# Expert products in four widths: TensorE branches on the token count of an expert

## Chip, cores, metric

The kernel runs on one core of a Trainium2 chip. The metric is device microseconds (us) of one execution, as the median of several runs; lower is better.

## The reference

Gated linear attention over 4 batches, 8 heads and 768 steps feeds a mixture of 8 experts, of which each token uses one, and a dense gated layer follows. What matters here is the mixture: 3,072 tokens of 384 features, each sent to the expert with the largest logit.

```python
logits = x @ w_gate
expert_idx = np.argmax(logits, axis=1)
...
for e in range(E):
    mask = expert_idx == e
    xe = x[mask]
    h = np.maximum(xe @ w1[e], 0.0)        # 384 -> 1024
    ye = h @ w2[e]                         # 1024 -> 384
    out[mask] = gate_w[mask, None] * ye
```

How many tokens an expert gets is known only when the attention has run. The inputs are drawn from a fixed seed, so the counts can be had from the reference itself: expert 0 gets 420 tokens, and the other seven, sorted, get 409, 404, 390, 387, 356, 354 and 352.

## The kernel before

The program has three stages. The attention, with the routing, runs to about 131 us of the profiled span; the experts run from there to about 369 us; the dense layer fills the rest. TensorE (PE) does the products; ScalarE (ACT) and VectorE (DVE) turn PSUM into the next operands; GpSimd (POOL) gathers tokens and splits some weights; SyncE (SP) issues the loads.

**Turns and capacities.** The experts are taken in turns. Turn 0 is expert 0, which starts on its first 192 tokens before the last batch has been routed; turns 1 to 7 are the others by falling count, sorted on the chip (`turns`). Since an instruction's size is fixed when the program is built, each turn works on as many columns (tokens) as its capacity in `CAPS` says: 448 for turn 0, then 464, 436, 420, 408, 396, 384, 370. A count above its capacity sends the whole call to a slow general path behind the `tc.If` at the end (line 1547).

**Products.** An expert is cut into 8 slices of 128 inner units. For slice `t` of 64, `F1` computes the inner units: nine products (`first`, line 1222), because each operand is split into a high and a low part and three of the four partial products are kept, over three blocks of 128 features; the result lies in a PSUM bank `hp`. ACT makes `hh` from it (line 1234) and DVE makes `hl` (line 1236). `S1` (line 1254) then multiplies `hh` and `hl` by the second weights, again nine products, into three accumulators `yb`, which are emptied into `yT` at the end of an expert (`y_store`, lines 1398 and 1400). A product is one weight load and one matmul of as many columns as the capacity.

**The order around the change** is written out by hand, in the loop from line 1478. It takes the slices in pairs (g0, g1): `F1` of g1, then weight splitting (`doubles`, `weights`), `F1` of the slice after the pair, transposes of gathered tokens for the next expert (`x_tile`, line 357), and `S1` of g0 and of g1. Each `F1` is followed at once by its `hh` on ACT and its `hl` on DVE, so those two sit in the middle of the other work of these in-order engines. `hp` alternates between two PSUM banks, 5 and 6 (`h_bank`); `hh` and `hl` have two buffers each. A few list steps (`late`: `offsets`, `turn_lists` and others) are dropped in, one per slice. `offsets` (lines 1322 to 1329) writes the first row of each turn into `regs`, from which engines load registers with `values_load`.

Of the kernel before, what the change touches and what calls it, by code (L numbers as in the profile page):

```python
# [35 lines left out]

CAPS = [448, 464, 436, 420, 408, 396, 384, 370]
CAP = max(CAPS)
CA = 192
NTILE = NT // 128  # L40
RING = 5
# [188 lines left out]
def gla_moe_kernel(  # L230
# [883 lines left out]
    with mctx:  # L1114
# [112 lines left out]
                        step()  # L1227

        def F1(t, c0, c1, mid=()):
            n = c1 - c0  # L1230
            hp = bank(h_bank(), [128, TM], "hp")[:, :n]
            first(wslot[slot1(t)], XT[t // NF], c0, c1, hp, mid)
            hh = mp.tile([128, TM], F32R, tag="hh", name="hh", bufs=2)
            nc.scalar.activation(hh[:, :n], hp, AF.Relu)  # L1234
            hl = mp.tile([128, TM], F32R, tag="hl", name="hl", bufs=2)
            nc.vector.scalar_tensor_tensor(  # L1236
                hl[:, :n], in0=hp, scalar=0.0, in1=hh[:, :n].bitcast(F32), op0=ALU.max, op1=ALU.subtract
            )
            hq[t, c0] = (hh, hl)
# [1 line left out]
        yb = {}  # L1241

        def S1(t, c0, c1, between=()):
            f = t % NF
            if f == 0 and c0 == 0:
                for dc in range(KD):
                    yb[dc] = bank(dc, [128, CAP], "yb")
            wh, wl = wslot[slot1(t)]
            hh, hl = hq.pop((t, c0))
            for dc in range(KD):  # L1250
                c = 384 + dc * 128
                i = 0
                for a, b_ in ((wh, hh), (wl, hh), (wh, hl)):
                    nc.tensor.matmul(  # L1254
                        yb[dc][:, c0:c1],
                        lhsT=a[:, c : c + 128],
                        rhs=b_[:, : c1 - c0],
                        start=(f == 0 and c0 == 0 and i == 0),
                        stop=(f == NF - 1 and i == 2),
                    )  # L1260
                    i += 1
                if dc < len(between):
                    between[dc]()
# [23 lines left out]
        for t in range(part):  # L1287
            if t == 2:
                add()
                w_split(4)  # L1290
                gather(0, (1, 2, 3))
            if t == 3:
                w_split(5)
            if t + 1 < part:
                F1(t + 1, 0, CA)
            for step in beside.get(t, []):
                step()
            if t == part - 2:
                x_tile(0, 1, CA - 128)
            if t == part - 1:  # L1300
                x_tile(0, 2, bk=4)
            S1(t, 0, CA, ([row[2], ranks_and, row[4]], [lambda: None, invert])[t] if t < 2 else [])
            if t == 0:
                row[5]()
                for step in placed:
                    step()
        x_tile(0, 3, bk=3)
        for t in range(4, 6):
            next_load()
        soon = [6, 7]  # L1310
        F1(*seq[0])
        lctx.close()
        wC = mctx.enter_context(tc.tile_pool(name="wC", bufs=1, reuse_waits="tile"))
# [8 lines left out]
        def offsets():  # L1322
            m = rt.tile([128, E, E], F32, tag="m8", name="m8", bufs=1)
            nc.vector.tensor_tensor(inc8, carry, e512, op=ALU.subtract)
            by_turn(inc8, m, cnt)
            nc.vector.tensor_tensor_scan(inc8, ones8, cnt, 0.0, op0=ALU.mult, op1=ALU.add)
            o = rt.tile([128, E], F32, tag="rk", name="o", bufs=1)
            nc.vector.tensor_tensor(o, inc8, cnt, op=ALU.subtract)
            nc.vector.tensor_copy(regs[:, 0:E], o)

        def read_offset(e):
            return nc.values_load(regs[0:1, e : e + 1], engines=(ET.Activation, ET.DVE), min_val=0, max_val=NT)
# [35 lines left out]
            nc.sync.dma_start(slot_d[0:NT].rearrange("(i p) o -> i (p o)", p=128), t[0:NTILE, 2, :])  # L1368

        def turn_lists():  # L1370
            t = bank(3, [4 * E, 128], "tr")
            nc.tensor.transpose(t, ttab, ident)
            nc.vector.tensor_copy(lists["to"], t)

# [7 lines left out]
            nc.sync.dma_start(lists["back"], slot_d[0:NT].rearrange("(i p) o -> i (p o)", p=128))  # L1382

        def turn_slots():
            t = bank(3, [128, NTILE], "tb")
            nc.tensor.transpose(t, lists["back"], ident[:NTILE, :NTILE])
            nc.vector.tensor_scalar(sidx, t, float(NT - 1), None, op0=ALU.min)

# [19 lines left out]
            nc.vector.tensor_tensor(xl[:, kc, :], src, xh[:, kc, :].bitcast(F32), op=ALU.subtract)  # L1408

        def F2(g):  # L1410
            if g >= NM * NF2:
                return
            if g == 0:
                HB[0], HBS[:] = -1, [4, 5, 6]
            m, f = divmod(g, NF2)
            hp = bank(h_bank(), [128, TM], "hp")
            first(wslot[slot2(f)], XT["m", m], 0, TM, hp)
            sg = mp.tile([128, TM], F32, tag="sg", name="sg", bufs=2)
# [58 lines left out]

        for i in range(0, len(seq), 2):
            (g0, *_), (g1, *_) = pair = seq[i : i + 2]
            F1(*seq[i + 1])  # L1480
            doubles(g0, 1)
            if g0 >= RING:
                weights(g0 + 3)
            doubles(g0)
            if g1 >= RING:
                weights(g1 + 3)
            F1(*seq[i + 2]) if i + 2 < len(seq) else F2(0)
            if soon:
                w_split(soon.pop(0))
                next_load()  # L1490
            for g in (g0, g1):
                e, f = divmod(g, NF)
                if f == NF - 2:
                    roff[e] = read_offset(e)
                if f in (1, 2, 3, 4):
                    x_tile(e + 1, f - 1, bk=7 if f % 2 else 4)
                if f in (2, 3, 4, 5):
                    gather(e + 2, (f - 2,))
                if g >= 2 and f < NF - 1 and late:
                    late.pop(0)()  # L1500
                if e == E - 1 and f in (2, 3, 4):
                    y_split(0, f - 2)
            doubles(g1)
            for g, c0, c1 in pair:
                S1(g, c0, c1)
                if g % NF == NF - 1:
                    y_store(g // NF)
        NG2 = NM * NF2
        checks = []
        for p in range(NP + 1):  # L1510
# [101 lines left out]
```

## Time and profile before

| what | value |
|---|---|
| median of 3 runs | 771.36 us (770.86 to 772.2) |
| the profiled execution | 772.25 us, of which 770.2 us are the span of the trace |
| PE busy | 756.6 us, 98% of the span |
| DVE, ACT, POOL busy | 61%, 48%, 21% |
| granted TensorE clock | 0.998 of full speed |

The page gives busy time by engine and by group of instructions, and the trace behind it can be asked for waits, for a stretch in order of time, or for one line. All times are counted from the start of the span. "PEld" is a weight load, "PEldq" or "DVEq" the sequencer of an engine, which handles branches, register loads and separate waits ahead of the work that the engine is doing.

### The profile page before, as it was taken

The page shows a single profiled execution, that of the slowest core. Times are in us where ns is not written, and L with a number is a line of the kernel's source. Part 1 is how long each engine was busy: PE and PEld are TensorE (multiplying, and loading weights), DVE is VectorE, ACT ScalarE, POOL GpSimd, SP SyncE. Part 2 cuts the span into 40 slices and gives each one's busy share as a digit, 9 for nine tenths or more (in the row PEclk, how much of TensorE's full clock was granted, in tenths as well). Part 3 has the DMA queues.
Part 4 walks back from the last instruction along what each step waited for, and adds up shares of the span by engine and source line. Part 5 has one row for each costly group of instructions (what it writes and reads, how often), then busy time and mean ns, then how long its engine had stood idle before and what let it go on. Part 6 is the DMA issues. An engine that isn't in the chain of part 4 may idle for free. (4 is left out here: it accounts for less than half of the span.)

```text
span 770.2 us, 13235 instructions
## 1 busy us (share of the span) xinstructions
PE 756.6 (98%) x5018; PEld 690.6 (90%) x5018; DVE 468.2 (61%) x771; ACT 366.1 (48%) x684; POOL 162.3 (21%) x207
## 2 busy tenths in 40 slices
PE   7999999999999999999999999999999999999997
PEld 6887877898999999999999899999989999898996
DVE  8989986657777787879688433333443333344222
ACT  1656566345554555555544334444554545334222
POOL 5764322321232222212121200020020001002002
PEclk9999999999999999999999999999999999999999
DMA  9797883544455465555111100030021101001001
GB/s 231 200 240 223 202 277 126 169 130 149 147 192 184 151 200 176 184 164 165 62 62 37 59 19 19 1 113 18 1 78 37 37 0 42 2 1 41 1 2 45
DMA packets 41776, 80.56 MB, mean 105 GB/s; under 512 B 5696, under 2 KB 19999, under 8 KB 41704
## 3 DMA queue, kind: packets, MB, share of 16 engines
q1 hardware_dynamic: 37704, 67.60, 29.4%
q0 software_dynamic: 4000, 12.03, 5.1%
q8 instruction: 41, 0.67, 0.4%
q14 instruction: 31, 0.25, 0.1%
HBM read 68.04 MB, written 9.47 MB: 101 GB/s over the span
## 5 line engine op out<-in xcount | busy, mean ns | idle before, releaser
L1222 PE MATMUL hp<-xh,wh 128*128 128x512 f32 (+10 forms) x498 | 182.4, 369 | 0.4 <-issue 0.4
L1222 PE MATMUL hp<-xh,wl 128*128 128x512 f32 (+10 forms) x498 | 182.1, 368 | 0.0
L1423 DVE TENSOR_TENSOR sg<-hp,sg 128x512 f32<-128x512 f32 (+1 forms) x97 | 66.5, 685 | 129.4 <-ACT sg L1422 128.9
L1222 PE MATMUL hp<-xl,wh 128*128 128x512 f32 (+10 forms) x498 | 129.4, 368 | 0.0
L1422 ACT ACTIVATE sg<-hp 128x512 f32<-128x512 f32 (+1 forms) x97 | 57.5, 593 | 119.1 <-PE hp L1222 114.1
L1222 PEld LDWEIGHTS hp<-xh,wh 128*128 128x128 f32 x498 | 93.6, 188 | 12.6 <-issue 1.1
L1222 PEld LDWEIGHTS hp<-xh,wl 128*128 128x128 f32 x498 | 93.7, 188 | 11.3
L1222 PEld LDWEIGHTS hp<-xl,wh 128*128 128x128 f32 x498 | 91.1, 188 | 12.6
L1234 ACT ACTIVATE hh<-hp 128x464 fp32r<-128x464 f32 (+9 forms) x70 | 34.1, 488 | 100.0 <-PE hp L1222 61.8
L1468 POOL DMA_INDIRECT out_dram<-o,sidx x24 | 23.3, 973 | 275.4 <-ACT o L1466 270.9
L1149 POOL TENSOR_TENSOR wl<-dx,wh 128x384 fp32r<-128x384 f32 x32 | 38.4, 1201 | 182.6 <-ACT wh L1146 182.6
L333 DVE TENSOR_TENSOR wl<-raw,wh 128x768 fp32r<-128x768 f32 x63 | 64.3, 1025 | 6.7 <-ACT wh L332 6.4
L1236 DVE SCALAR_TENSOR_TENSOR hl<-hp,hh 128x464 fp32r<-128x464 f32 (+9 forms) x70 | 38.5, 550 | 40.3 <-ACT hh L1234 38.2
L1434 DVE TENSOR_TENSOR hl<-sg,hh 128x512 fp32r<-128x512 f32 x49 | 33.9, 692 | 35.6 <-ACT hh L1433 34.2
L1433 ACT CAST hh<-sg 128x512 fp32r<-128x512 f32 x49 | 30.4, 621 | 49.9 <-DVE sg L1423 38.2
L1434 DVE TENSOR_TENSOR xl<-sg,xh 128x512 fp32r<-128x512 f32 (+1 forms) x48 | 32.7, 681 | 31.7 <-ACT xh L1433 21.3
L332 ACT CAST wh<-raw 128x768 fp32r<-128x768 f32 x64 | 51.5, 831 | 0.6 <-DMA raw<-in_wt_dram 0.5
L1254 PE MATMUL both<-hh,wh 128*128 128x420 f32 (+9 forms) x140 | 49.0, 350 | 0.0
L1254 PE MATMUL both<-hl,wh 128*128 128x420 f32 (+9 forms) x140 | 47.3, 338 | 0.0
L1254 PE MATMUL both<-hh,wl 128*128 128x420 f32 (+9 forms) x140 | 47.2, 337 | 0.0
L1433 ACT CAST xh<-sg 128x512 fp32r<-128x512 f32 (+1 forms) x48 | 29.3, 611 | 35.1 <-DVE sg L1423 32.0
L347 POOL DMA_INDIRECT xg<-x_d,gidx x29 | 32.7, 1127 | 39.7 <-PE xt L357 20.3
(363 smaller groups left out, 1647.4 us busy)
## 6 DMA issues: line engine op xcount, KB each, us to landing
raw<-in_wt_dram SPq DMA_DIRECT2D x64, 384.0 KB, 3.5
raw<-in_w_dram SPq DMA_DIRECT2D x32, 384.0 KB, 3.2
raw<-in_alpha_dram SPq DMA_DIRECT2D x16, 336.0 KB, 3.4
x_d<-xr SPq DMA_DIRECT2D x24, 192.0 KB, 1.9
E<-in_q_dram SPq DMA_DIRECT2D x18, 144.0 KB, 5.6
E<-in_k_dram SPq DMA_DIRECT2D x18, 144.0 KB, 3.1
E<-E POOLq DMA_DIRECT2D x18, 114.0 KB
E<-in_q_dram SPq DMA_DIRECT2D x4, 336.0 KB, 10.8
```

The costliest lines, as they stand in the source:

```text
L332: nc.scalar.copy(hi, raw[t])
L333: eng.tensor_tensor(lo, raw.pop(t), hi.bitcast(F32), op=ALU.subtract)
L347: nc.gpsimd.indirect_dma_start(out=x[:n], out_offset=None, in_=src, in_offset=bass.IndirectOffsetOnAxis(ap=idx[:n, i : i + 1], axis=0),)
L1149: nc.gpsimd.tensor_tensor(r["lo"], r["x"], r["hi"].bitcast(F32), op=ALU.subtract)
L1222: nc.tensor.matmul(hp, lhsT=a[:, kc * 128 : (kc + 1) * 128], rhs=x[:, kc, c0:c1], start=(i == 0), stop=(i == 8))
L1234: nc.scalar.activation(hh[:, :n], hp, AF.Relu)
L1236: nc.vector.scalar_tensor_tensor(hl[:, :n], in0=hp, scalar=0.0, in1=hh[:, :n].bitcast(F32), op0=ALU.max, op1=ALU.subtract)
L1254: nc.tensor.matmul(yb[dc][:, c0:c1], lhsT=a[:, c : c + 128], rhs=b_[:, : c1 - c0], start=(f == 0 and c0 == 0 and i == 0), stop=(f == NF - ...
L1422: nc.scalar.activation(sg[:, z], hp[:, z], AF.Sigmoid)
L1423: nc.vector.tensor_tensor(sg[:, z], hp[:, z], sg[:, z], op=ALU.mult)
L1433: nc.scalar.copy(hh[:, z], sg[:, z])
L1434: nc.vector.tensor_tensor(hl[:, z], sg[:, z], hh[:, z].bitcast(F32), op=ALU.subtract)
```

## The change

For turns 1 to 7 the program holds each group of products four times, in widths listed in `ARMS`, the last being the old capacity. PE loads the count of the turn into a register (once per turn) and, ahead of each group, compares it with the widths and jumps to the first that is large enough. There are nine groups in a turn: the first products of slice 0 alone, of slices 1 and 2, 3 and 4, 5 and 6, and of 7 alone, and the second products of four pairs. So there are 63 groups, each with three compares and four arms, and only PE's program has arms. On the other four engines each group leaves one unconditional jump.

```diff
+ARMS = [
+    [448],
+    [420, 432, 444, 464],
+    [404, 412, 420, 436],
+    [388, 396, 408, 420],
+    [376, 388, 396, 408],
+    [364, 376, 384, 396],
+    [344, 356, 368, 384],
+    [326, 342, 354, 370],
+]
...
+        def hold():
+            HB[0] = -1
+            for i in HBS:
+                t = bank(i, [128, CAP], "hp")
+                nc.vector.memset(t, 0.0)
+                held.append(t)
...
+                for t_ in yb.values():
+                    nc.vector.memset(t_[:, CAPS[0] :], 0.0)
...
+        HB[0], HBS[:] = -1, [5, 6, 3]
...
+            nc.vector.tensor_copy(regs[:, 9:16], cnt[:, 1:E])
+        count = {}
+        def sized(e, body):
+            if e not in count:
+                c = 8 + e if e else 8
+                count[e] = nc.values_load(regs[0:1, c : c + 1], engines=(ET.PE,), min_val=0, max_val=NT)
+            def arm(i):
+                if i == len(ARMS[e]) - 1:
+                    body(ARMS[e][i])
+                    return
+                with tc.If(count[e] <= ARMS[e][i]) as cmp:
+                    body(ARMS[e][i])
+                with cmp.Else():
+                    arm(i + 1)
+            arm(0)
...
         for i in range(0, len(seq), 2):
             (g0, *_), (g1, *_) = pair = seq[i : i + 2]
-            F1(*seq[i + 1])
+            todo = seq[i + 1 : i + 3]
+            for t, c0, c1 in todo:
+                F1_bank(t, c0)
...
+                    def firsts(w):
+                        for t, c0, c1 in mine:
+                            F1_products(t, c0, w)
+                    sized(e, firsts)
+            F1_inner(*seq[i + 1])
...
-            F1(*seq[i + 2]) if i + 2 < len(seq) else F2(0)
...
-            for g, c0, c1 in pair:
-                S1(g, c0, c1)
-                if g % NF == NF - 1:
-                    y_store(g // NF)
...
+                sized(e, seconds)
+            if i + 2 < len(seq):
+                F1_inner(*seq[i + 2])
+            else:
+                F2_inner(0)
+            if i == NF - 4:
+                hold()
+            if g1 % NF == NF - 1:
+                y_store(e)
```

Three more things move. `F1` falls into `F1_products` and `F1_inner`: the products of two slices now stand together, and `hh` and `hl` of the second slice come only after the second products of the pair. `hp` lives in three banks (5, 6, 3) that are allocated once and cleared by DVE (`hold`), since a narrow arm leaves the columns behind its width as they were; `turn_lists` and `turn_slots` go to bank 7 for it. ACT and DVE still work on the full capacity.

On PE, the first products of slice 0 of turn 1 (`xh`, `xl` the tokens, `wh_104`, `wl_105` its first weights) stood before between the last of turn 0 and the second products of turn 0:

```order
L1222 MATMUL hp<-xl_108,wh_2031 128x448 x3
L1222 MATMUL hp<-xh_2039,wh_104 128x464
L1222 MATMUL hp<-xh_2039,wl_105 128x464
L1222 MATMUL hp<-xh_2039,wh_104 128x464
L1222 MATMUL hp<-xh_2039,wl_105 128x464
L1222 MATMUL hp<-xh_2039,wh_104 128x464
L1222 MATMUL hp<-xh_2039,wl_105 128x464
L1222 MATMUL hp<-xl_2040,wh_104 128x464 x3
L1254 MATMUL both<-hh,wh_2029 128x448
L1254 MATMUL both<-hh,wl_2030 128x448
```

and now, with the load of the turn's count, the first compare and the first of the four arms:

```order
L1383 TENSOR_LOAD regs
L1383 ISA x2
L1389 COMPARE_AND_BRANCH
L1232 MATMUL hp<-xh_2039,wh_104 128x420
L1232 MATMUL hp<-xh_2039,wl_105 128x420
L1232 MATMUL hp<-xh_2039,wh_104 128x420
L1232 MATMUL hp<-xh_2039,wl_105 128x420
L1232 MATMUL hp<-xh_2039,wh_104 128x420
L1232 MATMUL hp<-xh_2039,wl_105 128x420
L1232 MATMUL hp<-xl_2040,wh_104 128x420 x3
L1389 UNCONDITIONAL_BRANCH
L1389 COMPARE_AND_BRANCH
```

What moved: the nine products stand inside an arm of 420 columns in place of 464, a register load and a compare ahead of them and a jump behind; three more arms of the same nine products follow in the program.

On DVE, at the end of turn 0 (`lists` is the token list, `wl` the low part of a weight, `xl` that of a token block; `hl` of 448 columns belongs to slices 6 and 7), before:

```order
L1236 SCALAR_TENSOR_TENSOR hl<-hp,hh 128x256
L333 TENSOR_TENSOR wl_105<-raw,wh_104 128x768
L1236 SCALAR_TENSOR_TENSOR hl<-hp,hh 128x448
L362 TENSOR_TENSOR xl_2040<-xt,xh_2039 128x3x80
L1373 COPY lists<-tr 32x128
L1236 SCALAR_TENSOR_TENSOR hl<-hp,hh 128x448
L333 TENSOR_TENSOR wl_2026<-raw,wh_2025 128x768
L333 TENSOR_TENSOR wl_99<-raw,wh_98 128x768
L1236 SCALAR_TENSOR_TENSOR hl<-hp,hh 128x464
L1332 TENSOR_LOAD regs
```

and now:

```order
L1272 SCALAR_TENSOR_TENSOR hl<-hp,hh 128x256 x2
L343 TENSOR_TENSOR wl_105<-raw,wh_104 128x768
L372 TENSOR_TENSOR xl_2040<-xt,xh_2039 128x3x80
L1438 COPY lists<-tr 32x128
L1272 SCALAR_TENSOR_TENSOR hl<-hp,hh 128x448
L1256 MEMSET hp 128x464 x3
L1389 UNCONDITIONAL_BRANCH
L1272 SCALAR_TENSOR_TENSOR hl<-hp,hh 128x448
L343 TENSOR_TENSOR wl_2026<-raw,wh_2025 128x768
L343 TENSOR_TENSOR wl_99<-raw,wh_98 128x768
L1389 UNCONDITIONAL_BRANCH
L1397 TENSOR_LOAD regs
```

What moved: `hl` of slice 6 stands behind the token block and the list, and three clears of `hp` follow it, ahead of `hl` of slice 7; a jump marks each group.

## Rows read from the trace of the kernel before

**Rows 1.** The page, parts 1 and 3: busy us, share, instructions; the instruction queue.

```profile
PE 756.6 (98%) x5018; PEld 690.6 (90%) x5018; DVE 468.2 (61%) x771; ACT 366.1 (48%) x684; POOL 162.3 (21%) x207
...
q8 instruction: 41, 0.67, 0.4%
```

**Rows 2.** Waits of PE from 131 to 370 us: total us, times, longest us.

```profile
PE xt L357 <- DMA xg<-x_d,gidx: 0.7, 1, 0.7
PE hp L1222 <- issue: 0.4, 1, 0.4
```

**Rows 3.** Engines in the stretch of turns 1 to 7: length, busy us (instructions) of PE, PEld, DVE, ACT, POOL.

```profile
165.00:370.00 205.00, 205.00 (x1125) 197.08 (x1124) 160.32 (x267) 109.06 (x204) 49.53 (x42) 1.00 0.52 168
```

**Rows 4.** Products of PE in turn 1, in order of time: start us, us.

```profile
177.38 0.38 PE L1254 MATMUL both<-hh,wl 128*128 128x464 f32 x1
...
180.94 0.37 PE L1222 MATMUL hp<-xh,wh 128*128 128x464 f32 x1
```

**Rows 5.** The same in turn 7.

```profile
352.96 0.33 PE L1254 MATMUL both<-hh,wh 128*128 128x370 f32 x1
...
355.51 0.33 PE L1254 MATMUL yb<-hh,wh 128*128 128x370 f32 x1
```

**Rows 6.** Line 1547, the branch at the end: ns min/median/max, first and last start us.

```profile
L1547 SPq EVENT_SEMAPHORE  x8: 17/17/17, 665.6 to 666.1; - x8
L1547 SPq COMPARE_BRANCH  x1: 53/53/53, 663.1 to 663.1; - x1
L1547 PEldq COMPARE_BRANCH  x1: 4015/4015/4015, 761.6 to 761.6; - x1
L1547 DVEq COMPARE_BRANCH  x1: 72/72/72, 765.0 to 765.0; - x1
...
L1547 POOLq COMPARE_BRANCH  x1: 54/54/54, 765.7 to 765.7; - x1
...
L1547 POOLq EVENT_SEMAPHORE  x1: 17/17/17, 765.9 to 765.9; - x1
```

**Rows 7.** The last product of PE, in order of time.

```profile
764.56 0.34 PE L1446 MATMUL ob<-wh,xl 128*128 128x384 f32 x1
```

**Rows 8.** DVE at its branch, in order of time.

```profile
764.94 0.37 DVE L1461 COPY o<-ob 128x200 f32<-128x200 f32 x1 [3.10 <-PE ob L1446]
```

**Rows 9.** Instruction queue of PE from 763 to 766 us: packets, MB, share of 16 engines.

```profile
q8 instruction: 1, 0.02, 1.9%
```

**Rows 10.** Line 357 from 160 to 178 us, the separate waits: count, ns min/median/max.

```profile
L357 PEldq EVENT_SEMAPHORE  x2: 51/819/1587, 160.4 to 173.1; - x2
```

**Rows 11.** PE while the longer of those waits runs, in order of time.

```profile
161.46 0.37 PE L1222 MATMUL hp<-xh,wh 128*128 128x448 f32 x1
161.67 0.36 PE L1222 MATMUL hp<-xh,wl 128*128 128x448 f32 x1
...
163.29 0.35 PE L357 MATMUL xt<-identr,xg 80*128 80x80 f32 x3
```

**Rows 12.** End of turn 0 on DVE, in order of time, with idle time ahead in brackets.

```profile
163.85 0.95 DVE L333 TENSOR_TENSOR wl<-raw,wh 128x768 fp32r<-128x768 f32 x1
165.33 0.62 DVE L1236 SCALAR_TENSOR_TENSOR hl<-hp,hh 128x448 fp32r<-128x448 f32 x1 [0.52 <-ACT hh L1234]
165.87 0.40 DVE L362 TENSOR_TENSOR xl<-xt,xh 128x240 fp32r<-128x240 f32 x1
166.18 0.27 DVE L1373 COPY lists<-tr 32x128 f32<-32x128 f32 x1
```

**Rows 13.** PE and ACT there, all engines in order of time.

```profile
164.75 0.54 ACT L1234 ACTIVATE hh<-hp 128x448 fp32r<-128x448 f32 x1 [1.98 <-PE yb L1254]
...
165.75 0.37 PE L1222 MATMUL hp<-xh,wh 128*128 128x448 f32 x1
```

**Rows 14.** Waits of DVE from 165 to 370 us: total us, times, longest us.

```profile
DVE hl L1236 <- ACT hh L1234: 32.6, 32, 1.9
```

**Rows 15.** The register load of PE ahead of the last branch.

```profile
L1540 PEldq TENSOR_LOAD <-regs x1: 492/492/492, 752.3 to 752.3; - x1
```

More of the change, by code (lines that the diff above doesn't have):

```diff
@@ L1229, in F1, with F1_products, F1_bank, F1_inner @@
         def F1(t, c0, c1, mid=()):
+            F1_bank(t, c0)
+            F1_products(t, c0, c1, mid)
+            F1_inner(t, c0, c1)
+        hps = {}
+        def F1_products(t, c0, c1, mid=()):
+            first(wslot[slot1(t)], XT[t // NF], c0, c1, hps[t, c0][:, : c1 - c0], mid)
+        held = []
+        def hold():
[4 more added lines that the diff above has]
+                held.append(t)
+        def F1_bank(t, c0):
+            if held:
+                HB[0] += 1
+                hps[t, c0] = held[HB[0] % len(held)]
+            else:
+                hps[t, c0] = bank(h_bank(), [128, CAP], "hp")
+        def F1_inner(t, c0, c1):
             n = c1 - c0
-            hp = bank(h_bank(), [128, TM], "hp")[:, :n]
-            first(wslot[slot1(t)], XT[t // NF], c0, c1, hp, mid)
+            hp = hps.pop((t, c0))[:, :n]
             hh = mp.tile([128, TM], F32R, tag="hh", name="hh", bufs=2)
@@ L1243, in S1, with S1_begin, S1_products @@
         def S1(t, c0, c1, between=()):
-            f = t % NF
-            if f == 0 and c0 == 0:
+            S1_products(t, c0, c1, S1_begin(t, c0), between)
+        def S1_begin(t, c0):
+            if t == 0 and c0 == 0:
                 for dc in range(KD):
                     yb[dc] = bank(dc, [128, CAP], "yb")
+            return hq.pop((t, c0))
+        def S1_products(t, c0, c1, inner, between=()):
+            f = t % NF
             wh, wl = wslot[slot1(t)]
-            hh, hl = hq.pop((t, c0))
+            hh, hl = inner
             for dc in range(KD):
@@ L1370, in turn_lists @@
         def turn_lists():
-            t = bank(3, [4 * E, 128], "tr")
+            t = bank(7, [4 * E, 128], "tr")
             nc.tensor.transpose(t, ttab, ident)
@@ L1384, in turn_slots @@
         def turn_slots():
-            t = bank(3, [128, NTILE], "tb")
+            t = bank(7, [128, NTILE], "tb")
             nc.tensor.transpose(t, lists["back"], ident[:NTILE, :NTILE])
@@ L1410, in F2, with F2_products @@
         def F2(g):
-            if g >= NM * NF2:
-                return
+            if g < NM * NF2:
+                F2_products(g)
+                F2_inner(g)
+        def F2_products(g):
             if g == 0:
@@ L1415, in F2, with F2_inner @@
             m, f = divmod(g, NF2)
-            hp = bank(h_bank(), [128, TM], "hp")
+            hps["m", g] = hp = bank(h_bank(), [128, TM], "hp")
             first(wslot[slot2(f)], XT["m", m], 0, TM, hp)
+        def F2_inner(g):
+            m, f = divmod(g, NF2)
+            hp = hps.pop(("m", g))
             sg = mp.tile([128, TM], F32, tag="sg", name="sg", bufs=2)
@@ L1479, in gla_moe_kernel @@
             (g0, *_), (g1, *_) = pair = seq[i : i + 2]
-            F1(*seq[i + 1])
+            todo = seq[i + 1 : i + 3]
+            for t, c0, c1 in todo:
+                F1_bank(t, c0)
+            for e in sorted({t // NF for t, _, _ in todo}):
+                mine = [x for x in todo if x[0] // NF == e]
+                if e == 0:
+                    for x in mine:
+                        F1_products(*x)
+                else:
+                    def firsts(w):
[3 more added lines that the diff above has]
+            F1_inner(*seq[i + 1])
             doubles(g0, 1)
@@ L1486, in gla_moe_kernel @@
                 weights(g1 + 3)
-            F1(*seq[i + 2]) if i + 2 < len(seq) else F2(0)
+            if i + 2 == len(seq):
+                F2_products(0)
             if soon:
@@ L1503, in gla_moe_kernel, with seconds @@
             doubles(g1)
-            for g, c0, c1 in pair:
-                S1(g, c0, c1)
-                if g % NF == NF - 1:
-                    y_store(g // NF)
+            e = g0 // NF
+            inner = {g: S1_begin(g, c0) for g, c0, c1 in pair}
+            def seconds(w):
+                for g, c0, c1 in pair:
+                    S1_products(g, c0, w, inner[g])
+            if e == 0:
+                for g, c0, c1 in pair:
+                    S1_products(g, c0, c1, inner[g])
+            else:
+                sized(e, seconds)
+            if i + 2 < len(seq):
+                F1_inner(*seq[i + 2])
+            else:
+                F2_inner(0)
[3 more added lines that the diff above has]
+                y_store(e)
         NG2 = NM * NF2
```

## Prediction

> **What bounds the kernel now.** I read the page first: PE is busy for 756.6 of 770.2 us, 98% of the span, and no other engine passes 61% [rows 1]. Busy time alone proves little for pipelined products, so the waits came second: from 131 to 370 us, where the experts run, PE waits once for 0.7 us and once for 0.4 us and hardly otherwise [rows 2]. The stretch of turns 1 to 7, 205 us long, shows PE busy in all of it at the full clock, 2.4 GHz (1.00), DVE in 160.32 us and ACT in 109.06 us [rows 3]. So the time of the expert stage is the number of products times the distance between two of them, and a shorter distance is a shorter kernel as long as nothing else becomes late.
>
> **What the arms save.** The distance follows the columns. In turn 1, at 464 columns, 17 distances take 180.94 - 177.38 = 3.56 us, 0.209 us each [rows 4]; in turn 7, at 370, 15 take 2.55 us, 0.170 us each [rows 5]. That is 0.0394 us for 94 columns, 0.42 ns a column. The counts of the reference's inputs (409, 404, 390, 387, 356, 354, 352) fall into the arms 420, 404, 396, 388, 364, 356 and 354, in place of 464, 436, 420, 408, 396, 384 and 370: 44 + 32 + 24 + 20 + 32 + 28 + 16 = 196 columns. Each turn makes 8 slices x 18 products = 144 products, so 196 x 144 = 28,224 columns go, at 0.419 ns **11.8 us**. Turn 2's count sits exactly on its arm; should the chip route one token otherwise there, the next arm gives back 8 x 144 x 0.42 ns = 0.5 us. ACT, DVE and the loads keep their sizes: nothing is saved there, and nothing needs to be.
>
> **What the branches cost.** Of the 63 groups each passes one to three compares and mostly one closing jump. What decides is whether PE's sequencer has time for them. At the end of the kernel it does its one branch at 761.6 us [rows 6] while the last product starts at 764.56 us [rows 7]: 3.0 us of work were already handed over. The expert stage shows the same lead at work: a separate wait of 1.587 us began at 160.4 us [rows 10], yet PE went from product to product through it, at 0.2 us distance [rows 11]. So what holds the sequencer for less than some 3 us is not seen by PE. A short jump is cheap where the trace has one: compare and branch take 54 ns on POOL, and its next instruction stands 0.2 us behind; on DVE the branch takes 72 ns [rows 6]. At 0.05 to 0.2 us each, at most four in a group are under 0.8 us of sequencer time against at least 9 x 0.17 us of products for a small group and 3 us for a large one. The register load took 0.49 us once [rows 15]; seven of them, one a turn, disappear under the lead as well. I take **0** for both; the upper end is in the rivals.
>
> **What the program's length costs.** PE runs 5,018 weight loads and 5,018 matmuls; queue 8 brought 41 packets of instructions [rows 1], which makes 245 a packet if it is PE's. The three arms that are not taken are 3 x 144 products a turn, 3,024 in all, 6,048 instructions or 25 packets more, on top of the ten that this stretch uses: one every 5.5 us. A packet keeps one of 16 DMA engines for 0.4% x 16 x 770.2 / 41 = 1.2 us [rows 1]. Fetched ahead, as they seem to be now (PE does not wait at packet borders, [rows 2]), they cost **0**. The lead hides what is left of a late one.
>
> **What DVE gets.** The clears of `hp` are new, and here PE does wait. At the end of turn 0, DVE is done with `wl` at 164.80 us [rows 12]. In the new order come the token block (0.40 us) and the list (0.27), to 165.47; `hl` of slice 6 (0.62), whose `hh` is there at 164.75 + 0.54 = 165.29 [rows 13], ends at 166.1; then the clear of bank 5. The trace has no clear of that size: I bound it by the 240-wide subtraction (0.40) and the 448-wide `hl` (0.62) and take 0.5, in between, since it writes as many columns but reads none. It ends at 166.6, and slice 7's products, which it releases, started at 165.75 [rows 13]. PE waits **0.9 us**, once; the bounds are 0.6 (`hl` on time, short clear) and 1.4 (the cast of the counts costs as much as the list, long clear). Behind it queue the rest of PE's work; the second and third clear run beside slice 7. The three clears of `yb`, 16 columns each, and the cast of the counts come early in turn 0; priced like the list copy (0.27 each) they are 1.1 us of DVE time beside products that do not wait for them, so 0, and 1.1 if `hl` were late by all of it.
>
> Elsewhere the move of `hl` is hidden: for the slice after the pair, `hh` still needs a buffer that the pair's first half frees, and its reader comes 18 products later, 3 us. DVE has 205 - 160 = 45 us free in the stretch, of which 32.6 are waits for `hh` [rows 14]; the shorter stretch takes 12, and 63 jumps of 72 ns take 4.5. On ACT, POOL and SP the jumps come to 3.4 us each (54 ns), beside work that fills half of ACT's time and a quarter of POOL's [rows 3]; SP's loads then go out at most that much later over the whole stretch. The third bank removes no wait of PE, since there is none. The two list transposes only change banks.
>
> **Sum.** 772.25 (profiled execution) - 11.8 + 0.9 = 761.35 us. The median of the runs is 0.89 us lower, so for it I predict **760.5 us**. Its own range is 758.8 (clear hidden, slope 2% up) to 763.
>
> **Rivals.**
>
> *A. Branches or late DVE work show through in part.* If a group costs 0.1 us of PE on average (a lead that is sometimes spent, an `hl` behind a full DVE), 63 x 0.1 = 6.3 us come back: 766.8. For it speaks that DVE is 78% busy and in order, and that a pair's two `hl` now stand side by side; against it the 45 us. Range 763 to 770.
>
> *B. A jump over a packet's border misses.* The one far jump that PE makes took 4.015 us [rows 6], with a packet of instructions fetched between 763 and 766 us [rows 9]. If the fetch ahead serves only code that is run through, each of the 25 borders inside skipped arms costs that, less a lead of 18 products x 0.18 = 3.2 us: 0.8 us x 25 = 20 us, **780.5 us**, slower. It decides from the point at which a miss is longer than the lead; SP's far jump took 2.5 us (663.1 to 665.6, [rows 6]), which the lead would hide. Against it: an arm group skips at most three arms, 108 instructions, less than half a packet, so the target is in the packet at hand or in the next. This is where the Trainium skill speaks against the change: "Runtime: NRT & Kernel Launch", section "Instruction fetch mechanics", has it that a taken branch breaks the sequential fetch when its target lies outside a window of two pages, and stalls until the page is there. Read strictly for every border that is jumped over, it gives the 780.5 us; POOL's short jump gives the 760.5. The far jump agrees with it; by the same sentence a jump this short stays inside, unless the next page is still on its way, and no row of this trace shows a short jump on PE.
>
> *C. PE's branch waits until its products are done.* Its branch did end, at 765.6 us, 0.7 us after the last product [rows 6, 7]. A bubble of 0.7 us at the compare and at the closing jump of 63 groups is 88 us, 848 us. Against it: the fetch that the branch set off fell into 763 to 766 us, and DVE's branch at 765.0 us ran beside a copy from 764.94 to 765.31 [rows 6, 8].
>
> *D. The arms are not the ones I think.* Were the count in the register above the narrow arms, each turn would take its old width: 772.25 + 0.9, against the median 772.3.
>
> **How the numbers follow.** The forecast gets 0.68, A 0.12, B 0.12, C 0.04, D 0.04. A measurement of this kernel can tell 0.2%, 1.5 us, from no change. The forecast and A are faster by more: 0.80. D is the same: 0.04. B and C are slower: 0.16. The range holds the forecast and A, 0.80 in all: 758.8 to 770 us. B, C and D, 0.20 together, are left out.
>
> **What would show it.** Right: matmuls of 420, 404, 396, 388, 364, 356 and 354 columns in the expert stage, the dense layer beginning some 11 us earlier, compares on PE's sequencer of about 0.1 us, some 66 packets of instructions, and one wait of `hp` for a clear on DVE of about 0.9 us. Wrong: compares or jumps of 2 to 4 us and waits of PE put down to issue (B), gaps of 0.7 us around each group (C), waits of PE for `hl` or `hh` (A), old widths (D).

## The result and the profile after

| | before | after |
|---|---|---|
| median of 4 runs each | 771.16 us (770.86 to 772.2) | **762.2 us** (760.28 to 764.2) |
| the profiled execution | 772.25 us | 761.62 us, span 759.6 us |

The ratio of the runs is 0.9877 (95% interval 0.9863 to 0.989): 1.2% faster, and the interval leaves out 1. That is 9.0 us against a forecast of 10.9. The sum was made for the profiled execution, 761.35 us, and that came out at 761.62.

The page of after, parts 1 and 3, answers to [rows 1]:

```profile
PE 745.3 (98%) x5018; PEld 682.3 (90%) x5018; DVE 466.8 (61%) x778; ACT 367.3 (48%) x684; POOL 167.0 (22%) x207
...
q8 instruction: 67, 1.10, 0.6%
```

The products are as many as before. PE's busy time is 11.3 us less, DVE and ACT stay within 1.4 us of what they were, POOL is 4.7 us up, and the instruction queue brought 26 packets more (forecast 25).

Products of turn 1 and of turn 7 in after, in order of time (start us, us), answer to [rows 4, 5]:

```profile
177.04 0.35 PE L1296 MATMUL both<-hh,wl 128*128 128x420 f32 x1
...
180.14 0.35 PE L1296 MATMUL yb<-hl,wh 128*128 128x420 f32 x1
```

```profile
342.53 0.32 PE L1296 MATMUL both<-hh,wh 128*128 128x354 f32 x1
...
345.41 0.32 PE L1232 MATMUL hp<-xh,wh 128*128 128x354 f32 x1
```

From the first to the last row stand 16 distances in turn 1, 0.194 us each, and 18 in turn 7, 0.160 us each; they were 0.209 and 0.170. PE's branches in after (nanoseconds min/median/max, first and last start us) answer to the one branch of [rows 6]:

```profile
L1389 PEldq COMPARE_BRANCH  x171: 64/176/1434, 166.7 to 355.8; - x171
```

The 171 are 63 closing jumps of 64 to 89 ns and 108 compares of 174 to 431 ns, but for two longer ones; 66 of the compares took more than 200 ns. Together they take 30.6 us of PE's sequencer, 0.49 us a group, and only one is longer than 1 us. The waits of PE from 165 to 353 us (total us, times, longest us), beside the none of the same turns before [rows 2]:

```profile
PE hp L1232 <- DVE hp L1256: 0.7, 1, 0.7
PE hp L1232 <- DVE wl L343: 0.4, 1, 0.4
PE both L1296 <- DVE hl L1272: 0.3, 1, 0.3
```

No wait is put down to issue or to a branch. The first is the forecast wait for the clear. DVE, then PE at that place, in order of time, answer to [rows 12, 13]:

```profile
163.50 0.27 DVE L1438 COPY lists<-tr 32x128 f32<-32x128 f32 x1
164.43 0.62 DVE L1272 SCALAR_TENSOR_TENSOR hl<-hp,hh 128x448 fp32r<-128x448 f32 x1 [0.66 <-ACT hh L1270]
165.23 1.43 DVE L1256 MEMSET hp<- 128x464 f32 x3 [0.17 <-DVE hl L1272]
```

```profile
164.73 0.28 PE L1296 MATMUL yb<-hl,wh 128*128 128x256 f32 x1
165.73 0.47 PE L1232 MATMUL hp<-xh,wh 128*128 128x448 f32 x1 [0.71 <-DVE hp L1256]
```

The list is done, DVE idles 0.66 us for `hh`, then come `hl` and three clears of 0.48 us (taken: 0.5). PE starts slice 7's first product 1.00 us behind the one ahead of it, where products of 256 columns stand 0.12 us apart: 0.88 us lost, forecast 0.9.

One more wait for a clear shows, which the forecast put at nothing. In turn 0, at 140.8 us, PE waited for the clears of `yb` (72 ns each, taken as 0.27 us each):

```profile
PE both L1296 <- DVE yb L1335: 0.3, 1, 0.3
```

**Where the time went.** The two profiled executions, cut at three products:

| | before | after | difference |
|---|---|---|---|
| start to the first 448-column product (slice 6 of turn 0) | 161.46 | 160.57 | -0.89 |
| from there to the first product of turn 1 | 6.12 | 7.08 | +0.96 |
| turns 1 to 7, to the first 512-column product | 196.09 | 185.55 | -10.54 |
| dense layer, to its last product | 400.89 | 400.73 | -0.16 |
| sum | 764.56 | 753.93 | -10.63 |

The first line differs by a microsecond or two between executions of one kernel. The second is the clear. The third is the arms: 11.8 forecast, 10.54 measured.

### The profile page after: what moved, and what is told of

The parts are those of the page before. It is cut to its first block, busy times and chain, and to the rows that moved or that the text cites. A ratio compares the mean times of both kernels' runs of the same rounds, so it can differ in the third digit from the quotient of the medians.

```text
span 759.6 us, 13436 instructions
## 1 busy us (share of the span) xinstructions
PE 745.3 (98%) x5018; PEld 682.3 (90%) x5018; DVE 466.8 (61%) x778; ACT 367.3 (48%) x684; POOL 167.0 (22%) x207
## 5 line engine op out<-in xcount | busy, mean ns | idle before, releaser
L1232 PE MATMUL hp<-xh,wh 128*128 128x512 f32 (+10 forms) x498 | 180.4, 365 | 1.1 <-DVE hp L1256 0.7
L1232 PE MATMUL hp<-xl,wh 128*128 128x512 f32 (+10 forms) x498 | 127.4, 364 | 0.0
L343 DVE TENSOR_TENSOR wl<-raw,wh 128x768 fp32r<-128x768 f32 x63 | 65.1, 1037 | 10.9 <-ACT wh L342 10.6
L1272 DVE SCALAR_TENSOR_TENSOR hl<-hp,hh 128x464 fp32r<-128x464 f32 (+9 forms) x70 | 37.8, 548 | 29.4 <-ACT hh L1270 29.2
L1296 PE MATMUL both<-hh,wh 128*128 128x396 f32 (+9 forms) x140 | 47.7, 341 | 0.3 <-DVE yb L1335 0.3
L1296 PE MATMUL both<-hl,wh 128*128 128x396 f32 (+9 forms) x140 | 46.0, 329 | 0.3 <-DVE hl L1272 0.3
L1296 PE MATMUL both<-hh,wl 128*128 128x396 f32 (+9 forms) x140 | 45.8, 327 | 0.0
L357 POOL DMA_INDIRECT xg<-x_d,gidx x29 | 34.5, 1188 | 42.1 <-PE xt L367 19.5
```

Of the source, the lines that this page charges most:

```text
L343: eng.tensor_tensor(lo, raw.pop(t), hi.bitcast(F32), op=ALU.subtract)
L357: nc.gpsimd.indirect_dma_start(out=x[:n], out_offset=None, in_=src, in_offset=bass.IndirectOffsetOnAxis(ap=idx[:n, i : i + 1], axis=0),)
L1232: nc.tensor.matmul(hp, lhsT=a[:, kc * 128 : (kc + 1) * 128], rhs=x[:, kc, c0:c1], start=(i == 0), stop=(i == 8))
L1272: nc.vector.scalar_tensor_tensor(hl[:, :n], in0=hp, scalar=0.0, in1=hh[:, :n].bitcast(F32), op0=ALU.max, op1=ALU.subtract)
L1296: nc.tensor.matmul(yb[dc][:, c0:c1], lhsT=a[:, c : c + 128], rhs=b_[:, : c1 - c0], start=(f == 0 and c0 == 0 and i == 0), stop=(f == NF - ...
```

## Experiments

Each kernel is the changed one with one edit; each was timed beside the kernel before on the same chip, and the ratio is to that. Three questions: do branches cost anything, where is the missing microsecond of the third line, and how many arms does the instruction fetch bear.

### Branches: all arms wide, and no branches at all

`e1_wide_arms` keeps branches, packets and clears, but every arm does the full capacity.

```diff
-                    body(ARMS[e][i])
+                    body(CAPS[e])
...
```

> All four arms of a group take the full capacity: the branches, jumps, extra packets of instructions, moved hl and the clears stay, no column is saved. Theory (branches and packets are hidden under the lead of PE's sequencer, the gain is the columns): 771.2 + 0.7 for the clear = 771.9 us, give or take 0.7, with PE free of waits in turns 1 to 7. Rival (branches or packets cost PE a little in every group, which is why the change gave 9.0 us and not 10.9): 774 us or more. Rival (late DVE work and loads, for which the shorter turns leave no slack): 771.9 as well, since the turns here are as long as before.

Measured: 773.6 us, ratio 1.0018 (1.0007 to 1.0029). The page, part 3, then PE's waits from 165 us to the dense layer:

```profile
q8 instruction: 67, 1.10, 0.6%
```

```profile
PE hp L1232 <- DVE hp L1256: 0.7, 1, 0.7
```

Turns 1 to 7 took 196.17 us, against 196.09 before: 171 branches and 26 packets cost 0.1 us in seven turns of this execution. What remains there is the wait for the clear. By the runs the kernel is 1.4 us slower than the one before beside it (772.23 us; 0.5 to 2.2 by the interval), where 0.7 was expected; the trace shows nothing but the clear for it.

`e2_no_branch` has no register load, no compare and no jump; each turn has the width that fits this input, written down.

```diff
+FIT = [448, 420, 404, 396, 388, 364, 356, 354]
...
-            arm(0)
+            body(FIT[e])
```

> No compare, no arm, no count: each group has the width that fits this input's counts, written into the program. All else is as changed. Theory: as the changed kernel, 762.2 give or take 1 us, with the same spread from run to run (760 to 764). Rival (branches cost a little in every group): about 760, the 2 us that were missing come back. Rival (the packets of skipped arms bring the spread): the spread falls to the 1.3 us of the kernel before.

Measured: 762.16 us, ratio 0.9872 (0.9851 to 0.9892), 41 packets, and the turns took 185.95 us. So the kernel with the branches (762.2) is as fast as one that knows the counts when it is built, and the missing microsecond isn't the branches'. This trace, without a branch, has the same two late waits of PE as after, for `wl` (at 311 us) and for `hl` (at 349 us):

```profile
PE hp L1233 <- DVE wl L344: 0.6, 1, 0.6
PE both L1297 <- DVE hl L1273: 0.5, 1, 0.5
```

The spread of its four runs is small (1.1 us), as the second rival has it; but the kernel before, with no arms, spread over 3.7 us in 17 runs on this chip, so the spread says nothing on the packets.

### The clear: two of three ahead of `hl`

`e4_clear_first` leaves slice 6 in its bank, clears the other two ahead of its `hl`, and gives slice 7 one of these.

```diff
+            if i == NF - 4:
+                hold()
+                hold_bank(1)
+                hold_bank(2)
...
-                hold()
+                hold_bank(0)
```

> The clears of the two banks that slice 6 does not use go ahead of its hl, and slice 7 takes one of them; only the third clear stays behind hl. Theory: the wait of 0.7 us for the clear goes, 761.5 us, no wait of hp for a clear. Rival (what follows is late by DVE or loads anyway, so the 0.7 us turn up again further on): 762.2 us.

Measured: 761.22 us, ratio 0.9853 (0.9836 to 0.987). The wait for the clear is gone from the trace; its only wait of PE in turns 1 to 7:

```profile
PE both L1299 <- DVE hl L1275: 0.3, 1, 0.3
```

From the first 448-column product to turn 1 it took 6.10 us, as before (6.12; 7.08 in after), and the wait did not turn up again further on: turns 1 to 7 took 184.63 us. So the clear was DVE's order alone, as its term had it. By the medians the gain is 1.0 us beside the first runs of the changed kernel, and none beside those of the next section.

### The missing microsecond: loads, or DVE's order

In the profiled execution of after, ACT waited 7.3 us for raw weights:

```profile
ACT wh L342 <- DMA raw<-in_wt_dram: 7.3, 8, 2.0
```

and PE was held in turns 6 and 7 by `wl`, which is made from them, and by `hl`. Whether both hang on the loads is the question here. Four kernels ran together: the changed one again, five load buffers for four, the old place of `hl`, and five buffers with the early clears.

`c_after`:

> The changed kernel once more, unedited, so that the kernels beside it are compared on the same chip. Both theories: 762.2 us or within 1 us of it, ratio 0.987 to 0.989, with PE's stalls of 0.5 to 1 us in turns 6 and 7 again.

Measured: 760.96 us (760.66 to 762.52), ratio 0.9861 (0.9842 to 0.9879). In this execution the turns took 184.63 us without a wait of PE; its one wait from 163 us on is for the clear, ahead of turn 1:

```profile
PE hp L1232 <- DVE hp L1256: 0.7, 1, 0.7
```

So the stall is not a property of the kernel: it came in one of two profiled executions. Nor is ACT's wait for raw weights enough to bring it, since that was 8.9 us here. Their turns 1 to 5 have the same lengths, 29.4, 27.9, 27.4, 26.8 and 25.0 us; turns 6 and 7 took 25.3 and 23.7 in the one, 24.6 and 23.5 in the other. That is 0.9 us, less than the 1.4 of the expectation.

`e5_raw5` (the smaller padding serves this input's counts only):

```diff
+PAD = 24
...
-    wraw = ctx.enter_context(tc.tile_pool(name="wraw", bufs=4))
+    wraw = ctx.enter_context(tc.tile_pool(name="wraw", bufs=5))
...
-        yT = wC.tile([128, KD, NT + CAP], F32, name="yT")
+        yT = wC.tile([128, KD, NT + PAD], F32, name="yT")
...
```

> The changed kernel with five buffers for raw weights in place of four; the room comes from the padding of yT, 24 columns in place of 464, which is enough for the counts of this input alone. Theory, that the ring of raw buffers is what runs short once the turns are shorter (the loads wait for a buffer, ACT's split waits for the load, DVE's wl for ACT, PE for wl): PE's stalls in turns 6 and 7 go, together about 1.4 us, so about 760.9 us, and ACT's wait for raw weights falls from 7.3 us to under 3. Rival, that DVE in order is the limit, whatever the loads do: 762 as before, and the stalls stay, with DVE busy ahead of them.

Measured: 761.99 us (761.38 to 762.51), ratio 0.9869 (0.9849 to 0.9889). As the theory had it, ACT's waits for raw weights are gone, and the turns took 184.01 us without a stall; but the unedited kernel beside it, 0.6 us longer in its turns, had no stall either. The theory was wrong on the time. PE's longest wait from 140 to 165 us in this kernel, and the same transposes here and in after:

```profile
PE xt L368 <- DMA xg<-x_d,gidx: 1.3, 1, 1.3
```

```profile
153.89 0.45 PE L368 MATMUL xt<-identr,xg 128*128 128x128 f32 x3 [1.26 <-DMA xg<-x_d,gidx]
```

```profile
152.21 0.37 PE L367 MATMUL xt<-identr,xg 128*128 128x128 f32 x3
```

With a fifth buffer SP issues four weight loads from 147.29 us on, in 6.8 us, where after issues three from 146.44 in 7.3, and the gathered tokens come late: the gather issued beside these loads landed after 5.8 us, in after 3.8. What the turns gained, this wait took back. That the load's bytes delay the gather was not tried by itself.

`e6_hl_early`:

```diff
-            if i + 2 == len(seq):
+            if i + 2 < len(seq):
+                F1_inner(*seq[i + 2])
+            else:
                 F2_products(0)
+                F2_inner(0)
...
-            if i + 2 < len(seq):
-                F1_inner(*seq[i + 2])
-            else:
-                F2_inner(0)
```

> The changed kernel with hh and hl of the slice after the pair back at their old place, ahead of the transposes and of the second products of the pair; all else as changed. Theory, that the later place of hl costs nothing and the loads make the stalls: 762.2 us within 0.7, the stalls in turns 6 and 7 of the same size, and ACT's wait of hh for yb back near 34 us from 6. Rival, that hl behind the second products is what comes late in turns 6 and 7: the wait for hl at 348 us goes, 0.5 to 1 us faster. Second rival, that the old place holds up the token block and the next weights on ACT and DVE, which the shorter turns cannot bear: 1 to 3 us slower.

Measured: 762.47 us (761.02 to 763.73), ratio 0.9881 (0.9863 to 0.9899). In its profiled execution the turns took 184.46 us, and ACT's wait of `hh` for `yb` was 21.7 us from 165 to 353 us, against 4.7 in after (34 expected). The median is 1.5 us above that of `c_after`, which would suit the second rival (1 to 3 us slower); but the intervals of the two ratios overlap, and in the trace the turns are no longer than there. The one loss to be seen is at the clear, which stands behind the token block and the list here: PE waited 1.1 us for it. So the new place of `hl` costs no time that these runs can tell.

`e8_both` joins the edits of `e4_clear_first` and `e5_raw5`.

> Two clears ahead of hl of slice 6, in banks that this slice does not use, and five raw buffers in place of four. If the waits for the clear and for the loads are separate and both show in full: 762.2 - 0.9 - 1.4 = about 759.9 us, with no wait of PE over 0.4 us between 165 and 353 us. If the clear alone counts (the loads' stall is DVE's): 761.2, as with the clears alone.

Measured: 760.41 us (759.71 to 763.14), ratio 0.9855 (0.9833 to 0.9878); no wait of PE from 163 to 353 us, turns 184.01 us, and again 1.0 us of waiting for the gather at 153 us. It has the lowest median, but 0.55 us below the changed kernel of the same chip, with ranges that overlap, is no finding. The medians of this section all lie between 760.28 and 762.78 us, over which eight of the changed kernel's own nine runs scatter (median of the nine 761.62).

What shortens turns 6 and 7 is not settled. One execution of each kernel was profiled:

| | turn 6, us | turn 7, us |
|---|---|---|
| after | 25.33 | 23.69 |
| `c_after` | 24.57 | 23.51 |
| `e2_no_branch` | 25.50 | 23.91 |
| `e4_clear_first` | 24.38 | 23.71 |
| `e6_hl_early` | 24.83 | 23.09 |
| `e5_raw5` and `e8_both`, each | 24.38 | 23.09 |

Five buffers bring both turns to their shortest, twice of two. But turn 6 is as short in `e4_clear_first` and turn 7 in `e6_hl_early`, both with four. So the loads may have a part in the stall, and DVE's order too.

### How many arms the instruction fetch bears

Arms that are never taken stand behind the four: eight more (`e3_twelve_arms`), four more (`e7_eight_arms`), two (`e10_six_arms`), one (`e11_five_arms`). They do the full capacity; the widths that are run stay the same.

```diff
+ARMS = [a + [c + 512 * k for k in range(1, 9)] if len(a) > 1 else a for a, c in zip(ARMS, CAPS)]
...
-                    body(ARMS[e][i])
+                    body(min(ARMS[e][i], CAPS[e]))
```

> Each group of turns 1 to 7 gets eight more arms of the full capacity behind the four, which are never taken; the same arms as before are. A closing jump of a two-slice group now passes 8 to 11 arms, 300 to 420 instructions, more than a packet of 245. Theory with packets fetched one ahead only: the target is not there, 4.0 us less a lead of 3.2, 0.8 us in each of 63 groups, some 50 us: 812 us; if skipped packets must all be fetched on the way, 100 us or more. Rival (many packets are held and fetched ahead, so a jump of two packets is still covered): 762 to 765 us.

Measured: 871.74 us, ratio 1.1292 (1.1264 to 1.132). The branches, and PE's longest waits from 170 to 463 us:

```profile
L1390 PEldq COMPARE_BRANCH  x171: 64/224/6886, 169.5 to 465.3; - x171
```

```profile
PE hp L1233 <- issue: 21.8, 12, 3.7
PE both L1297 <- issue: 14.4, 8, 4.0
PE xt L368 <- issue: 9.6, 5, 3.1
```

The picture that rival B was to show: 64 branches over 1 us, 222 us in all, and PE out of instructions. Two causes fit it: a jump that is too far for what has been fetched, or too many packets to fetch in the time. The next two runs tell them apart; the second, `e9_arms_front`, puts the eight dead arms ahead of the four, so that no jump passes more than three arms.

```diff
+ARMS = [list(range(1, 9)) + a if len(a) > 1 else a for a in ARMS]
...
-                    body(ARMS[e][i])
+                    body(ARMS[e][i] if ARMS[e][i] > 8 else CAPS[e])
```

> The changed kernel with four more arms per group behind the four, at full capacity and never taken: eight arms, with the widths that are run unchanged. The arms add about 25 packets of PE's instructions again, some 92 in all, 60 of them in the expert stage. Theory 1, a rate: the fetch brings at best one packet per 3.1 us (the shortest gap between two packets with twelve arms). 60 x 3.1 = 186 us is just the 184 to 186 us of the stage, so about 762 to 770 us. Theory 2, a distance: what costs is the closing jump over the arms behind the one that was run, as soon as it is longer than the packet that is fetched ahead. Over seven arms of 36 instructions that is 252, about one packet, against 1.6 packets with twelve arms: some 30 to 40 jumps of 4 us less the lead of 3 us, so 790 to 800 us. Rival B is dead: 762.

> Twelve arms again, as many instructions and packets as in the run with twelve arms, but the eight that are never taken stand ahead of the four: each group fails eight compares, each of which jumps over one arm, and the closing jump passes three arms at most. Theory 1, a rate: about as slow as twelve arms with the dead ones behind, 860 to 880 us, and the long branches are now compares. Theory 2, the distance of a jump: no jump is longer than 108 instructions, so none waits for a packet as the long ones did; eight more compares of 64 to 176 ns are 0.5 to 1.4 us a group, mostly inside the lead, so 762 to 790 us.

Measured: eight arms 828.52 us, ratio 1.0712 (1.0665 to 1.076); twelve with the dead ones ahead 941.07 us, ratio 1.2187 (1.2161 to 1.2213). Of the latter the page, part 3, then the branches, then the longest waits from 170 to 531 us:

```profile
q8 instruction: 134, 2.20, 1.0%
```

```profile
L1390 PEldq COMPARE_BRANCH  x675: 69/208/4579, 167.2 to 534.6; - x169
```

```profile
PE hp L1233 <- issue: 63.4, 25, 5.0
PE both L1297 <- issue: 25.6, 13, 3.3
```

No time that either theory gave came true: eight arms were to take 762 to 770 us by the rate and 790 to 800 by the distance, the dead arms ahead 860 to 880 and 762 to 790. Yet with short jumps throughout, the latter has 81 branches of over 1 us and is the slowest of all: the distance of the jump is not the cause. With the dead arms behind, the closing jump even helps: 117 packets came where all the code makes 133 (8 arms x 8.25 more than 67), so some 16 were passed over unfetched; ahead, 134 came. The added compares, 0.2 us each, also take sequencer time; how much of the 941 us is theirs was not separated. At 3.65 us a packet, the 17 packets that the stage has more than with the dead arms behind are 62 of the 69 us between the two. My count for eight arms was short (four arms more are 33 packets, not 25: 100 came) and so was the price, since 3.1 us is close to the shortest usual gap between two packets, not to the mean.

With 3.6 to 3.8 us a packet from these runs, two more were forecast, near the point at which the fetch should just keep up.

> The changed kernel with two more arms per group, never taken, behind the four. Theory, a rate of fetching: in the expert stage the runs with eight and twelve arms took 3.6 to 3.8 us for each packet of PE's instructions, whatever the jumps. A pair's group with six arms is 6 x 36 = 216 instructions, at 245 a packet 0.88 packets, so 3.2 us of fetching; its 18 products take 18 x 0.193 = 3.5 us in turn 1 and 18 x 0.160 = 2.9 us in turn 7. So turns 1 to 3 run free and turns 5 to 7 are short of instructions by some 0.2 to 0.3 us for each of the 8 slices of a turn: 5 to 7 us, about 768 us (764 to 774), with 83 packets in all and PE's waits for issue in the late turns alone. Rival, a threshold on the length of an arm group (one packet): 216 is below 245, so nothing shows, 762.

> The changed kernel with one more arm per group, never taken, behind the four. Theory, a rate of fetching at 3.6 to 3.8 us a packet: a pair's group is 180 instructions, 0.73 packets, 2.7 us of fetching against 2.9 to 3.5 us of products: nothing shows, 762 us within 1.5, with 75 packets in all. Rival, that every packet costs something (by the runs with eight and twelve arms): 8 packets more are 8 x 2 = 16 us, 778.

Measured: five arms 762.92 us, ratio 0.9883 (0.9866 to 0.9899); six 780.74 us, ratio 1.0106 (1.0072 to 1.0141). Both rivals fall: the 16 us for eight more packets do not come at five arms, and a group of 216 instructions, shorter than a packet, does cost. Their branches, five arms and then six:

```profile
L1390 PEldq COMPARE_BRANCH  x171: 64/176/2439, 166.7 to 356.9; - x171
```

```profile
L1390 PEldq COMPARE_BRANCH  x171: 64/207/4007, 171.8 to 375.5; - x171
```

Five arms may not be quite free: 16 of their branches took over 1 us, PE waited 0.6 us for issue, and turns 5 and 7 took 25.42 and 24.70 us, where each execution with the same widths and fewer arms took 24.99 and at most 23.91. That is some 2 us in all, too little for the medians to tell.

Six arms lost more than the 5 to 7 us expected: the turns took 200.6 us, 16 more than in `c_after`, and turn 2 (31.3 us for 27.9) and turn 6 (31.2 for 24.6) lost most, not the last three evenly. An average per group hides that groups of 9 and of 18 products, transposes and late `wh` on ACT come in clumps; that this is the reason was not shown. Of PE's waits in this stage 4.6 us are put down to issue and 6.3 us to ACT, and how the second hang on the first was not followed. The two longest:

```profile
PE hp L1233 <- issue: 3.6, 3, 1.4
PE hp L1233 <- ACT wh L343: 1.5, 1, 1.5
```

Its profiled execution also entered turn 1 some 4 us late, with nothing in the changed place before; that was not followed.

All runs side by side; the packets are those of queue 8 from the first product of turn 1 to the first of 512 columns:

| arms a group | packets | turns 1 to 7, us | us a packet | branches over 1 us | median, us |
|---|---|---|---|---|---|
| 1 (before) | 9 | 196.1 | 21.8 | none | 771.16 |
| 4 (after) | 33 | 185.6 | 5.6 | 1 | 762.2 |
| 5 | 41 | 186.6 | 4.6 | 16 | 762.92 |
| 6 | 50 | 200.6 | 4.0 | 36 | 780.74 |
| 8 | 66 | 251.6 | 3.8 | 48 | 828.52 |
| 12, dead behind | 82 | 292.6 | 3.6 | 64 | 871.74 |
| 12, dead ahead | 99 | 361.2 | 3.65 | 81 | 941.07 |

From eight arms on, the stage is its packets times 3.6 to 3.8 us, though the products that run are the same in all rows but the first; with four arms it has 5.6 us for each packet.

## Why the prediction was right, and where not

- **What the arms save: right, 2 to 3% too large.** All seven widths were as named. `e1_wide_arms` against `c_after`, the same program at two sets of widths, gives 196.17 - 184.63 = 11.54 us for 28,224 columns, 0.409 ns each where 0.419 was read from two turns. The profiled execution of after, with its stall, gives 10.6 us in place of 11.54.
- **Branches: right.** A group's 0.49 us of sequencer time lies inside the lead; `e1_wide_arms` shows 0.1 us for all. A compare was priced too low: 174 ns at least, and over 200 ns in 66 of 108, where 0.05 to 0.2 us was taken from other engines' branches. The lead covers that too.
- **The program's length: 0 is right, its reason only in part.** 25 packets more, one every 5.5 us, came out as 26 and 5.6. But the cover that I named, a packet's 1.2 us of transfer and the lead, is not what decides. The fetch has a pace, hardly ever under 3.0 us a packet and 3.6 to 3.8 when it is the limit, and four arms use 33 x 3.65 = 120 of 185 us of it. The rows of before could not show that pace: there a packet comes every 21.8 us.
- **Rival B** has its symptom and not its mechanism. The Trainium skill ("Runtime: NRT & Kernel Launch", section "Instruction fetch mechanics") lays the stall on a taken branch whose target is outside the two pages at hand. Here stalls came without a far target: `e9_arms_front`, with no jump over 108 instructions, is slower than `e3_twelve_arms` with jumps of up to 396 by 69 us. In this kernel what counts is the code that must be fetched, run or not. The same section of the Trainium skill calls the crossing to the next block mostly hidden; that held here, to within some 2 us in the stage, up to a packet every 4.6 us, and not at 4.0.
- **What DVE gets: right in its size, partly by luck.** The clear cost 0.88 us against 0.9 (0.48 us a clear against 0.5), and `e4_clear_first` takes it away. But the 0.9 held 0.18 us for an `hl` that starts late behind the token block and the list (165.47 for 165.29 us), and `hl` was not late: DVE was idle for 0.66 us ahead of it. In its place DVE idled 0.17 us between `hl` and the first clear, which the sum did not have. The clears of `yb`, put at 0, cost PE one wait of 0.3 us. Moving `hl` cost nothing that can be measured (`e6_hl_early`).
- **Rival A, in part.** "ACT, DVE and the loads keep their sizes: nothing is saved there, and nothing needs to be" was too sure. In some executions PE waits in turns 6 and 7, which made them 0.9 us longer in after than in `c_after`. With five load buffers it is gone in both executions, which speaks for the loads; that they are the cause is not shown, since `c_after` and `e6_hl_early` come near it with four. The wait comes without branches too (`e2_no_branch`), so of the two halves of rival A it is the late work, not the branches. The sum had no term for it.
- **The sum.** 761.35 forecast, 761.62 in the first profiled execution and 761.87 in the second. That the first comes within 0.3 us is partly luck: the arms gave 1.3 us less than forecast there, and the start, which has no term, was 0.9 us shorter. The second needs no such help: its start was 0.3 us longer, its turns 11.5 us shorter. The lower end of the range, 758.8, is 0.6 us below what its two named causes give (760.5 - 0.9 - 0.2 = 759.4); nothing hangs on it. That the medians differ by 9.0 us and not 10.9 in the first set is mostly scatter: in the second it was 771.79 - 760.96 = 10.8.

## What to carry to other kernels

Where PE is the bound and each product costs its columns, arms of different widths behind a compare give the saving of static widths, as long as the sequencer has its lead. Before adding arms, count the instructions of all of them, not of the one that runs: packets in the stage times the fetch pace must stay well under the stage, with some 20% left for clumps (150 of 187 us cost some 2 at most here, 182 of 185 cost 16; the rule rests on these two points). And when a buffer is added to remove a late wait, look at what its earlier transfer runs into: here, it seems, the gather of turn 0.

## What was not expected of the hardware

- PE's instruction fetch leaves hardly ever less than 3.0 us between the starts of two packets of 16 KB, and 3.6 to 3.8 us on average when it is the limit. Of the 303 gaps from 165 us on in the three kernels with eight and twelve arms 14 are shorter; the seven under 2 us, 0.3 to 1.05 us, are all in `e3_twelve_arms`, where jumps leap over packets. Beyond that limit the time grows with dead code: eight never-taken arms cost 109 us, 14% of the kernel.
- The clock followed. With twelve arms, where PE idles between groups, the mean granted clock of the stage fell to 0.91 (dead arms behind) and 0.83 (ahead), a mean over stretches at either level, 2.4 and 1.2 GHz, from 1.00 in the changed kernel. What the lower clock itself added to the time was not separated. The row is of the slowest, from 170 to 531 us (length, then busy us of PE, PEld, DVE, ACT, POOL, then the clock):

```profile
170.00:531.00 361.00, 242.85 (x1076) 223.50 (x1076) 155.69 (x257) 103.90 (x193) 48.09 (x40) 0.83 0.32 98
```

- On PE's sequencer a closing jump takes 64 ns at least and a compare 174. On the other four engines the trace of `e3_twelve_arms` has 63 jumps each, of 32 to 53 ns; the trace of the changed kernel records none there, so their cost in it can't be read, but no wait points at them.
